# The share of v in the routing logits: embeddings as stationary operand in four column tiles, keys moving, then transposed back

## The chip, the core and the metric

The kernel runs on one core of a Trainium2 chip. A core has TensorE (PE, matrix products; its weight loads are listed as PEld), VectorE (DVE), ScalarE (ACT), GpSimd (POOL) and SyncE (SP, which here issues most DMA transfers). The metric is the device time of one execution in microseconds; less is better.

## What is computed

Windowed causal attention, then two mixture-of-experts layers in a row, each of which sends a token to its best expert.

```python
scores = np.where(mask, scale * q @ k.T + bias, -1e9)   # 4 batches, 8 heads, 576 tokens, head size 64
attn   = softmax(scores)                                # window of 128
x      = (attn @ v), heads side by side                 # 2304 tokens x 512
# layer 1, 8 experts of 512 x 1024 x 512
logits = normalised(x) @ normalised(expert_emb).T / tau
out[t] = gate[t] * (relu(x[t] @ w1[e]) @ w2[e]),  e = argmax(logits[t])
# layer 2: the same with logits = x @ w_gate
```

The logits of layer 1 are linear in the attention output before its normalisation. So the kernel doesn't compute them from x: it multiplies v by the embeddings first, one product for each head, and lets the attention weights sum these 8 numbers (E = 8) per token and head together with v.

## The kernel before

Attention goes through 80 units: 4 batches, each in two halves of 4 heads; in a half 5 blocks of queries (four of 128, one of 64) times 2 pairs of heads. Loop step s starts unit s and carries earlier units on: `scores` of unit s (q times k, tile `ps_s`, L604), exponentials of unit s-1 on ScalarE (tile `e`, L631), transposes of unit s-2 on PE (`ps_t`, L638), their copy to SBUF by ScalarE for unit s-3 (`et`, L644), split into two halves of the window by GpSimd (L656, L658), product with v of unit s-5 (`pv`, `ps_o`, L677 for the first block, L679 and L680 for the others), normalisation of unit s-6 on VectorE. A matrix product in fp32 is two records in the trace, each with its weight load; a transpose is one.

The schedule is manual: on each engine, and in each DMA queue, instructions stand in the order in which the code issues them. Semaphores order the engines among themselves. A transfer also waits for an earlier one: there are eight completion semaphores for the transfers (`DMAHW0` to `DMAHW7`), taken in turn over both queues, and a transfer waits for the one that used its semaphore before it.

`vts` holds, for two batches, v by tokens: for each of five blocks and 8 heads 64 values, a one, and 8 places for the product of v and the embeddings. A transfer (`load_v`, L486) fills v and the ones. `v_logits` fills the 8 places: `load_vT` (L490) brings a block of v transposed (4 groups of two heads, 128 partitions, 128 tokens); for each group one product with the block as stationary operand and the embeddings `enT` as moving operand (L523, tile `ps_v`, 128 tokens by 128 columns of which 16 are used); ScalarE's `put` (L509) moves the used ones to `vts`. `enT` has in each group the embeddings of the even head in the upper 64 rows, those of the odd head in the lower.

For the first batch `v_logits` is advanced by one `yield` in each step, after the exponentials and before the transposes; its first three vT blocks are loaded from SP's queue ahead of everything, the others by ScalarE's queue. For the later batches it is advanced at the end of each step, with some steps' pause between blocks. PSUM tiles of `ps_m` (two buffers, tag `misc`) are shared by `v_logits`, the gate and the transposes of the expert stage.

After attention the tokens are sent to a table by expert (L287), and the experts run, 16 of them in turn (L985 to L987 are their products).

Of the kernel before, what the change touches and what calls it, by code (L numbers as in the profile page):

```python
# [7 lines left out]
F32 = mybir.dt.float32  # L8
# [3 lines left out]
AF = mybir.ActivationFunctionType  # L12
# [6 lines left out]
B, H, S, D = 4, 8, 576, 64  # L19
T, DM, E, FF = B * S, H * D, 8, 1024  # L20
NB = 5
QB = [128, 128, 128, 128, 64]
# [3 lines left out]
KD, KF = DM // 128, FF // 128  # L26
# [11 lines left out]
NW = 4  # L38
JOIN = 224
NT = 5  # L40
NOV = 26

PAUSE = object()
# [41 lines left out]
class _Kernel:  # L85
# [16 lines left out]
    def consts(self):  # L102
# [18 lines left out]
        nc.gpsimd.iota(t("exbase", [128, E]), pattern=[[TP, E]], base=0, channel_multiplier=0, **it)  # L121
        nc.gpsimd.iota(t("ovt", [128, NOV]), pattern=[[1, NOV]], base=0, channel_multiplier=0, **it)
        nc.gpsimd.iota(t("ovs", [128, NOV]), pattern=[[128, NOV]], base=0, channel_multiplier=0, **it)
        yield
# [6 lines left out]
        for m in range(2):  # L131
# [18 lines left out]
            t(f"proc{m}", [128, E])  # L150
            t(f"oei{m}", [1, 2, NOV], I32)
            yield
# [7 lines left out]
    def gate_consts(self, rows, psum):  # L160

        nc, c, t = self.nc, self.c, self.const
        es = rows.tile([128, DM], F32, tag="row", name="es")[:E]
        en, e0 = t("en", [E, 1]), self.e0
        nc.scalar.activation(es, e0, AF.Square, accum_out=en)
        nc.gpsimd.tensor_tensor(en, en, c["half"][:E, :1], op=ALU.pow)
        yield
        nc.vector.tensor_scalar(en, en, 1e-6, None, ALU.add)
        nc.vector.tensor_tensor(en, en, c["taub"], op=ALU.mult)
        nc.vector.reciprocal(en, en)  # L170
        nc.vector.tensor_scalar(es, e0, en, None, ALU.mult)
        yield
        ep = psum.tile([128, 512], F32, tag="misc", name="ep")
        for kk in range(KD):
            nc.tensor.transpose(ep[:, kk * E : kk * E + E], es[:, kk * 128 : kk * 128 + 128], c["ident"][:E, :E])
        yield
        enT = t("enT", [128, KD * 2 * E + 128 - 2 * E])
        nc.vector.memset(enT, 0.0)
        for z in range(2):
            nc.vector.tensor_copy(enT[64 * z : 64 * z + 64, : KD * 2 * E].rearrange("p (k e) -> p k e", k=KD)[:, :, E * z : E * z + E],  # L180
                                  ep[64 * z : 64 * z + 64, : KD * E].rearrange("p (k e) -> p k e", k=KD))

    def bias(self, pool):
# [26 lines left out]
    def gate(self, m, l, nt, meta, slots, fix=None, valid=None, skip=None, lag=None, norm=None):  # L210
# [6 lines left out]
        def s3(name, dt=F32):  # L217
            return pool.tile([128, NT, E], dt, tag=f"g_{name}", name=f"g_{name}")[:, :nt]

        def s2(name, dt=F32):  # L220
            return pool.tile([128, NT], dt, tag=f"g_{name}", name=f"g_{name}")[:, :nt]

# [3 lines left out]
        def be(a):  # L226
            return a.unsqueeze(1).to_broadcast([128, nt, E])
# [31 lines left out]
        nc.tensor.matmul(pos, lhsT=c["ones"], rhs=be(acc), start=False, stop=True)  # L259
        cnt = pp[:, NT * E : NT * E + E]  # L260
        nc.tensor.matmul(cnt, lhsT=c["ones"], rhs=new, start=True, stop=True)
# [131 lines left out]
    def beyond(self, m, cnt):  # L393
# [4 lines left out]
        def t(name, shape, dt=F32):  # L398
            return gp.tile(shape, dt, tag=f"ov_{name}", name=f"ov_{name}")

        def by_e(x):
            return x.unsqueeze(2).to_broadcast([128, E, NOV])

        def by_t(x):
            return x.unsqueeze(1).to_broadcast([128, E, NOV])

        ov, nov = t("ov", [128, E]), t("nov", [128, E])
        og, o2 = t("og", [128, E, NOV]), t("o2", [128, E, NOV])
        nc.vector.tensor_tensor(ov, cnt, proc, op=ALU.subtract)
# [40 lines left out]
    def attention(self):  # L450
        nc, c = self.nc, self.c
        fifo, par = self.fifo, self.par
        W = D + 1 + E
        with ExitStack() as st:
            def P(name, bufs, **kw):
                return self.pool(st, name, bufs, **kw)

            kp = P("at_k", 1)
            wk, wk3, wk4 = P("at_w", 2), P("at_w3", 3), P("at_w4", 4)
            ps_s, ps_t, ps_o = P("ps_s", 2, space=PSUM), P("ps_t", 2, space=PSUM), P("ps_o", 2, space=PSUM)  # L460
            ps_m, rows = self.ps_m, self.rows
# [5 lines left out]
            vts = [kp.tile([128, NB * H * W + 128 - W], F32, name=f"vt{i}") for i in range(2)]  # L467

            vTs = {}

            def load_qk(i, y):

                b, f = halves[i]
                for a in range(2):
                    nc.sync.dma_start(qz[i % 2][y][64 * a : 64 * a + 64, a, :S], self.q[b, 2 * f + y, 64 * a : 64 * a + 64])
                nc.sync.dma_start(kz[i % 2][y], self.k[b, 2 * f + y])
# [7 lines left out]
            def load_v(b, x):  # L484
                n = QB[x]
                nc.sync.dma_start(vts[b % 2][:n, x * H * W : (x + 1) * H * W], self.v[b, x * 128 : x * 128 + n])  # L486

            def load_vT(b, x, eng=nc.scalar):
                vTs[b, x] = vT = wk3.tile([128, KD, 128], F32, tag="vT", name="vT")
                eng.dma_start(vT[:, :, : QB[x]], self.vT[b, :, :, x * 128 : x * 128 + QB[x]])  # L490

            def load(i):
                for y in range(2):
# [7 lines left out]

            def v_logits(b):

                for x in range(3):
                    if (b, x) not in vTs:
                        load_vT(b, x)
                def put(x, ps):
                    to = vts[b % 2][: QB[x], x * H * W : (x + 1) * H * W].rearrange("p (h w) -> p h w", h=H)
                    nc.scalar.activation(to[:, :, D + 1 :].rearrange("p (g z) e -> p g z e", z=2),  # L509
                                         ps[: QB[x]].rearrange("p (g f) -> p g f", g=KD)[:, :, : 2 * E].rearrange("p g (z e) -> p g z e", z=2), AF.Copy)  # L510

                for x, n in enumerate(QB):
                    for _ in range(4 if b and x % 2 == 0 else 0):
                        yield
                    if x:
                        put(x - 1, ps)
                        if x + 2 < NB:
                            load_vT(b, x + 2)
                    vT = vTs.pop((b, x))
                    ps = ps_m.tile([128, 512], F32, tag="misc", name="ps_v")  # L520
                    for g in range(KD):

                        nc.tensor.matmul(ps[:n, g * 128 : g * 128 + n], lhsT=vT[:, g, :n],  # L523
                                         rhs=c["enT"][:, g * 2 * E : g * 2 * E + n], start=True, stop=True)
                    yield
                put(NB - 1, ps)
                yield

            nc.vector.memset(self.const("half", [128, NB]), 0.5)
            ssqs = [self.const(f"ssq{i}", [128, NB]) for i in range(2)]  # L530
# [1 line left out]
            nc.scalar.activation(ssqs[0], ssqs[0], AF.Exp)  # L532
            load_qk(0, 0)
            self.gate_loads(rows)
            for x in range(2):
                load_v(0, x)
                load_vT(0, x, nc.sync)
            load_qk(0, 1)
            for x in range(2, 4):
                load_v(0, x)  # L540
                if x == 2:
                    load_vT(0, 2, nc.sync)
            load_v(0, 4)
            clear_q(0, 0, nc.vector)
            ident = self.const("ident", [128, 128])
# [35 lines left out]
            def gate_start():  # L581

                yield from gate
                yield
                yield from v_logits(0)

            vl = gate_start()
# [155 lines left out]
            for s in range(N + 7):  # L743
# [3 lines left out]
                if s < N:  # L747
                    i, j, p = units[s]
                    if (j, p) == (0, 1) and i and i + 1 < 2 * B:
                        par.add(load(i + 1))  # L750
                    if (j, p) == (3, 1) and halves[i] in [(b, 0) for b in range(B - 1)]:
                        par.add(load_vs(halves[i][0] + 1))
                    if (j, p) == (0, 0) and halves[i][1] == 1 and i + 1 < 2 * B:
                        par.add(v_logits(halves[i][0] + 1))
# [59 lines left out]
    def load_x(self, m, C, tab, key, src):  # L814
# [3 lines left out]
        nf, w = divmod(C, 128)  # L818
        meta = self.mp.tile([128, NT, 2], I32, tag="meta", name="meta")[:, :nt]
        if w:  # L820
# [6 lines left out]
        if m == 0:  # L827
            valid = self.mp.tile([128, NT], F32, tag="valid", name="valid")[:, :nt]
            skip = self.mp.tile([128, NT], F32, tag="skip", name="skip")[:, :nt]
        xj = None  # L830
# [439 lines left out]
```

## Time and profile before

| | |
|---|---|
| time, median of 3 runs | 723.21 us (722.36 to 723.77) |
| the profiled execution | 724.26 us, span 722.5 us |
| PE busy | 694.9 us, 96% of the span |
| DVE, ACT, POOL busy | 64%, 47%, 31% |
| granted clock of PE, mean | 0.986 |
| attention | about the first 185 us |

The time of an execution lies a little above its span, which goes from the first to the last instruction. Busy shares are means over stages of different kind, so they only say where to look.

### The profile page before, as it was taken

What the parts mean: (1) busy time and instruction counts of PE and PEld (TensorE: products, weight loads), DVE (VectorE), ACT (ScalarE), POOL (GpSimd) and SP (SyncE); (2) the same over time, 40 slices, a digit from 0 to 9 for tenths busy, and PEclk for the clock granted to TensorE, in tenths of its full rate; (3) what the DMA queues carried; (4) which work ended last, traced back from release to release, by engine and by line L of the source; (5) the groups of instructions that cost most, each with busy time, mean ns of one, the idle gap of its engine ahead of it and who ended that gap; (6) DMA issues with size and microseconds to landing.
All of it is one profiled execution on the core that took longest, in us unless ns stands there. A gap on an engine that the chain in (4) does not pass through costs nothing.

```text
span 722.5 us, 15371 instructions
## 1 busy us (share of the span) xinstructions
PE 694.9 (96%) x5215; PEld 673.5 (93%) x5215; DVE 462.7 (64%) x1611; ACT 339.2 (47%) x841; POOL 222.7 (31%) x372
## 2 busy tenths in 40 slices
PE   6799999998999999999999998999999999999996
PEld 5799999997989899999999998999999999999996
DVE  7366667587686756675767776763655555666671
ACT  3355455566425343544455453522544444455551
POOL 5233443545335222223233124133212212211311
PEclk9999999999998999999999999999999999999999
DMA  8725646431418545356545475016544444554700
GB/s 230 197 84 180 139 134 192 121 151 51 163 28 285 176 142 211 105 216 161 202 157 148 161 194 217 23 31 239 223 152 171 161 173 141 217 209 147 257 21 14
DMA packets 45135, 112.41 MB, mean 156 GB/s; under 512 B 15000, under 2 KB 23448, under 8 KB 36820
## 3 DMA queue, kind: packets, MB, share of 16 engines
q1 hardware_dynamic: 27588, 87.83, 35.8%
q0 software_dynamic: 8448, 18.93, 9.0%
q10 hardware_dynamic: 8976, 3.93, 2.4%
q8 instruction: 87, 1.43, 0.8%
q14 instruction: 36, 0.29, 0.2%
HBM read 97.58 MB, written 15.93 MB: 157 GB/s over the span
## 4 chain that ended last, share of the span: by engine, by line
PE 77%; DMA 11%; DVE 4%; issue 4%; POOL 2%; SPq 1%; ACT 0%; POOLq 0%; ACTq 0%; DVEq 0%
PE ps L985 17%; PE ps L986 16%; PE ps L987 16%; PE ps_s L604 8%; DMA xr<-xs,meta 7%; PE ps_o L679 4%; PE ps_o L680 4%; PE tpx L858 2%; PE ps_t L638 2%; PE ps_v L523 2%; PE tpy L931 2%; DVE wlo L805 2%; PE ps L982 1%; PE tpy L943 1%; DMA vt<-in_v 1%
## 5 line engine op out<-in xcount | busy, mean ns | idle before, releaser
L805 DVE TENSOR_TENSOR wlo<-raw,whi 128x512 fp32r<-128x512 f32 x256 | 169.5, 687 | 72.6 <-ACT whi L802 62.7
L985 PE MATMUL ps<-xh,whi 128*128 128x240 f32 (+12 forms) x544 | 165.7, 305 | 1.6 <-DVE tot L1050 0.9
L985 PE MATMUL ps<-hh,whi 128*128 128x240 f32 (+11 forms) x544 | 165.7, 305 | 0.0
L986 PE MATMUL ps<-hl,whi 128*128 128x240 f32 (+10 forms) x544 | 161.4, 297 | 0.9 <-DVE hl L1084 0.9
L986 PE MATMUL ps<-xl,whi 128*128 128x240 f32 (+10 forms) x544 | 161.1, 296 | 0.9 <-DVE xl L862 0.5
L987 PE MATMUL ps<-hh,wlo 128*128 128x240 f32 (+10 forms) x544 | 161.3, 297 | 0.0
L987 PE MATMUL ps<-xh,wlo 128*128 128x240 f32 (+10 forms) x544 | 160.7, 295 | 0.5 <-issue 0.5
L802 ACT ACTIVATE whi<-raw 128x512 fp32r<-128x512 f32 x256 | 151.5, 623 | 3.0 <-DMA raw<-in_moe_w 3.0
L1079 ACT ACTIVATE hh<-ps 128x256 fp32r<-128x256 f32 (+10 forms) x136 | 57.2, 421 | 114.3 <-PE ps L987 107.4
L985 PEld LDWEIGHTS ps<-xh,whi 128*128 128x128 f32 x544 | 102.7, 189 | 2.2 <-ACT yT L1116 1.1
L986 PEld LDWEIGHTS ps<-hl,whi 128*128 128x128 f32 x544 | 103.5, 190 | 1.3 <-DVE hl L1084 1.3
L986 PEld LDWEIGHTS ps<-xl,whi 128*128 128x128 f32 x544 | 102.7, 189 | 1.8 <-DVE xl L862 1.0
L985 PEld LDWEIGHTS ps<-hh,whi 128*128 128x128 f32 x544 | 103.4, 190 | 0.5 <-ACT hh L1079 0.2
L987 PEld LDWEIGHTS ps<-xh,wlo 128*128 128x128 f32 x544 | 102.6, 189 | 1.0 <-issue 0.9
L987 PEld LDWEIGHTS ps<-hh,wlo 128*128 128x128 f32 x544 | 103.3, 190 | 0.1
L844 POOL DMA_INDIRECT xr<-xs,meta x50 | 53.8, 1076 | 157.7 <-DMA meta<-tab 106.1
L1084 DVE SCALAR_TENSOR_TENSOR hl<-ps,hh 128x256 fp32r<-128x256 f32 (+10 forms) x136 | 63.3, 467 | 60.2 <-ACT hh L1079 53.5
L1116 ACT ACTIVATE yT<-ps 128x256 f32<-128x256 f32 (+10 forms) x68 | 28.8, 423 | 126.0 <-PE ps L987 106.0
L604 PE MATMUL ps_s<-kz,qz 128*128 128x256 f32 (+1 forms) x320 | 81.5, 379 | 5.4 <-DMA kz<-in_k 5.4
L604 PEld LDWEIGHTS ps_s<-kz,qz 128*128 128x128 f32 x320 | 55.0, 195 | 9.5 <-DVE vt L551 5.4
L287 POOL DMA_INDIRECT out<-y,meta x26 | 31.6, 1215 | 93.0 <-DVE y L944 88.2
L631 ACT ACTIVATE e<-z,mn 128x128 f32<-128x128 f32 x160 | 54.6, 391 | 5.5 <-DVE mn L622 5.3
(205 smaller groups left out, 1034.0 us busy)
## 6 DMA issues: line engine op xcount, KB each, us to landing
raw<-in_moe_w SPq DMA_DIRECT2D x64, 1024.0 KB
vt<-in_v SPq DMA_DIRECT2D x16, 292.0 KB
qz<-in_q SPq DMA_DIRECT2D x32, 144.0 KB
kz<-in_k SPq DMA_DIRECT2D x16, 288.0 KB
xs<-xt SPq DMA_DIRECT2D x16, 256.0 KB
vT<-in_vT ACTq DMA_DIRECT2D x13, 256.0 KB
xr<-xs,meta POOLq DMA_INDIRECT x50
vT<-in_vT SPq DMA_DIRECT2D x3, 256.0 KB
```

The source lines that it names most:

```text
L287: k = self.nc.gpsimd.indirect_dma_start(dst, bass.IndirectOffsetOnAxis(ap=idx, axis=0), src, None, bounds_check=last, oob_is_err=False)
L604: nc.tensor.matmul(ps[:, a, k1:], lhsT=qz[i % 2][p][:, a, j * 128 : j * 128 + 128], rhs=kz[i % 2][p][:, m0 + k1 : m0 + 256], start=True, s ...
L631: nc.scalar.activation(e[:, a], z[:, a], AF.Exp, bias=mn[:, a : a + 1], scale=-1.0)
L679: nc.tensor.matmul(o, lhsT=e0[:, a], rhs=cols(j - 1), start=True, stop=False)
L802: nc.scalar.activation(hi[:, sl], rw[:, sl], AF.Copy)
L805: (eng or eng2).tensor_tensor(lo[:, sl], rw[:, sl], hi[:, sl].bitcast(F32), op=ALU.subtract)
L844: k = nc.gpsimd.indirect_dma_start(x[:n], None, src, bass.IndirectOffsetOnAxis(ap=meta[:n, i, 0:1], axis=0), bounds_check=src.shape[0] - 1 ...
L985: nc.tensor.matmul(ps[:, :v], lhsT=ah, rhs=Bh[:, kk, :v], start=kk == 0, stop=False)
L986: nc.tensor.matmul(ps[:, :w], lhsT=ah, rhs=Bl[:, kk, :w], start=False, stop=False)
L987: nc.tensor.matmul(ps[:, :w], lhsT=al, rhs=Bh[:, kk, :w], start=False, stop=kk == kn - 1)
L1079: nc.scalar.activation(hh[:, mm], ps, AF.Relu)
L1084: nc.vector.scalar_tensor_tensor(hl[:, mm], ps, 0.0, hh[:, mm].bitcast(F32), op0=ALU.max, op1=ALU.subtract)
```

## The change

The two operands of the v products change places. `enT` becomes 4 groups of 32 columns (16 of them used) and is the stationary operand; the block of v transposed moves. Group g writes PSUM partitions 32g to 32g+31, so that four products fill the 128 partitions of one tile, each in its own tile of 32 columns of the array. The result then has tokens along the free dimension. So ScalarE copies it to SBUF (`vl`, L524), PE transposes it in pieces of 128 tokens (L528, tile `ps_vt`), and `put` (L536) moves the used parts to `vts` as before. Blocks are 256, 256 and 64 tokens wide; vT has two buffers in place of three. The pipeline in `v_logits` becomes one step longer: products, then copy and transposes, then `put`.

```diff
+PM = 512
...
-        enT = t("enT", [128, KD * 2 * E + 128 - 2 * E])
+        enT = t("enT", [128, KD, 32])
         nc.vector.memset(enT, 0.0)
...
+            VB = ((0, 256), (256, 256), (512, 64))
+
             def load_vT(b, x, eng=nc.scalar):
-                vTs[b, x] = vT = wk3.tile([128, KD, 128], F32, tag="vT", name="vT")
-                eng.dma_start(vT[:, :, : QB[x]], self.vT[b, :, :, x * 128 : x * 128 + QB[x]])
+                k0, n = VB[x]
+                vTs[b, x] = vT = wk.tile([128, KD, 256], F32, tag="vT", name="vT")
+                eng.dma_start(vT[:, :, :n], self.vT[b, :, :, k0 : k0 + n])
...
             def v_logits(b):
 
-                for x in range(3):
+                for x in range(2):
                     if (b, x) not in vTs:
                         load_vT(b, x)
...
-                for x, n in enumerate(QB):
-                    for _ in range(4 if b and x % 2 == 0 else 0):
+                pss = {}
+
+                def products(x):
+
+                    n = VB[x][1]
+                    vT = vTs.pop((b, x))
+                    pss[x] = ps = ps_m.tile([128, PM], F32, tag="misc", name="ps_v")
+                    for g in range(KD):
+                        nc.tensor.matmul(ps[32 * g : 32 * g + 32, :n], lhsT=c["enT"][:, g], rhs=vT[:, g, :n], start=True, stop=True)
+
+                def turned(x):
+                    n = VB[x][1]
+                    sb = wk.tile([128, 256], F32, tag="vl", name="vl")
+                    nc.scalar.activation(sb[:, :n], pss[x][:, :n], AF.Copy)
+                    pss[x] = ps = ps_m.tile([128, PM], F32, tag="misc", name="ps_vt")
+                    for y in range(0, n, 128):
+                        k = min(128, n - y)
+                        nc.tensor.transpose(ps[:k, y : y + 128], sb[:, y : y + k], c["ident"])
+
+                def put(x):
+                    k0, n = VB[x]
+                    ps = pss.pop(x)
+                    for y in range(0, n, 128):
...
+                for x in range(len(VB) + 2):
+                    for _ in range(3 if b and x < len(VB) else 0):
                         yield
-                    if x:
-                        put(x - 1, ps)
-                        if x + 2 < NB:
+                    if x >= 2:
+                        put(x - 2)
+                    if 0 < x <= len(VB):
+                        turned(x - 1)
+                    if x < len(VB):
+                        products(x)
+                        if x + 2 < len(VB):
                             load_vT(b, x + 2)
...
-            for x in range(2):
-                load_v(0, x)
-                load_vT(0, x, nc.sync)
+            load_v(0, 0)
+            load_vT(0, 0, nc.sync)
+            load_v(0, 1)
             load_qk(0, 1)
-            for x in range(2, 4):
-                load_v(0, x)
-                if x == 2:
-                    load_vT(0, 2, nc.sync)
+            load_v(0, 2)
+            load_vT(0, 1, nc.sync)
+            load_v(0, 3)
             load_v(0, 4)
```

On PE, steps 3 to 6 of the first batch, before (`ps_s` scores, `ps_t` transposes, `ps_v` products of v, `ps_o` product with v):

```order
L604 MATMUL ps_s<-kz_114,qz_110 128x256 x2
L523 MATMUL ps_v<-enT,vT 128x128 x4
L638 MATMUL ps_t<-ident,e 128x128 x2
L604 MATMUL ps_s<-kz_114,qz_110 128x192 x2
L523 MATMUL ps_v<-enT,vT 128x128 x4
L638 MATMUL ps_t<-ident,e 128x128 x2
L604 MATMUL ps_s<-kz_115,qz_111 128x256 x2
L523 MATMUL ps_v<-enT,vT 128x128 x4
L677 MATMUL ps_o<-vt_118,et 128x128 x2
```

The same place on PE in the changed program (its line numbers are 22 higher from the scores on):

```order
L626 MATMUL ps_s<-kz_114,qz_110 128x256 x2
L519 MATMUL ps_v<-vT,enT 32x256 x4
L660 MATMUL ps_t<-ident,e 128x128 x2
L626 MATMUL ps_s<-kz_114,qz_110 128x192 x2
L528 MATMUL ps_vt<-ident,vl 128x128 x2
L519 MATMUL ps_v<-vT,enT 32x256 x4
L660 MATMUL ps_t<-ident,e 128x128 x2
L626 MATMUL ps_s<-kz_115,qz_111 128x256 x2
L528 MATMUL ps_vt<-ident,vl 128x128 x2
L519 MATMUL ps_v<-vT,enT 32x64 x4
L699 MATMUL ps_o<-vt_118,et 128x128 x2
```

The last products of the batch have moved one step ahead, and transposes of ScalarE's copy now stand between scores and products.

On ScalarE at that place, before, from the exponentials of step 3 on (the brackets name the semaphores that an instruction waits for; DMAHW7 was last used by the load of the last block of v):

```order
L631 ACTIVATE e<-z,mn 128x128 [waits DVE_49] x2
L644 ACTIVATE et<-ps_t 128x256 [waits PE_49]
L631 ACTIVATE e<-z,mn 128x128 [waits DVE_49] x2
L509 ACTIVATE vt_118<-ps_v 128x8x8 [waits DMAHW5_49]
L490 DMA vT<-in_vT 128x4x128 [waits DMAHW7_49,DMAHW6_49]
L644 ACTIVATE et<-ps_t 128x256 [waits PE_49]
```

And in the changed program (DMAHW3 was last used by the load of v's third block):

```order
L653 ACTIVATE e<-z,mn 128x128 [waits DVE_49] x2
L494 DMA vT<-in_vT 128x4x64 [waits DMAHW6_49,DMAHW3_49,PE_49]
L666 ACTIVATE et<-ps_t 128x256 [waits PE_49]
L653 ACTIVATE e<-z,mn 128x128 [waits DVE_49] x2
L524 ACTIVATE vl<-ps_v 128x256
L666 ACTIVATE et<-ps_t 128x256 [waits PE_49]
L653 ACTIVATE e<-z,mn 128x128 [waits DVE_49] x2
L536 ACTIVATE vt_118<-ps_vt 128x8x8 [waits DMAHW5_49]
L536 ACTIVATE vt_118<-ps_vt 128x8x8 [waits DMAHW7_49]
L524 ACTIVATE vl<-ps_v 128x256
```

The only load of vT that ScalarE still issues in the first batch has moved ahead by one copy and one pair of exponentials, waits for PE's first products instead of the last block of v, and is followed by copies of the products.

On SP's queue, loads for the first batch, before:

```order
L486 DMA vt_118<-in_v 128x584
L490 DMA vT<-in_vT 128x4x128
L486 DMA vt_118<-in_v 128x584
L490 DMA vT<-in_vT 128x4x128
L475 DMA qz_111<-in_q 64x576 x2
L476 DMA kz_115<-in_k 128x576
L486 DMA vt_118<-in_v 128x584
L490 DMA vT<-in_vT 128x4x128
L486 DMA vt_118<-in_v 128x584
L486 DMA vt_118<-in_v 64x584
```

After:

```order
L487 DMA vt_118<-in_v 128x584
L494 DMA vT<-in_vT 128x4x256
L487 DMA vt_118<-in_v 128x584
L476 DMA qz_111<-in_q 64x576 x2
L477 DMA kz_115<-in_k 128x576
L487 DMA vt_118<-in_v 128x584
L494 DMA vT<-in_vT 128x4x256
L487 DMA vt_118<-in_v 128x584
L487 DMA vt_118<-in_v 64x584
```

Three blocks of vT have become two of double width, so that 512 of 576 tokens are loaded from here in place of 384; up to the second pair of heads' k the bytes are the same.

## Rows read from the trace of the kernel before

**Rows 1.** The page: busy time, and the chain's shares by engine.

```profile
PE 694.9 (96%) x5215; PEld 673.5 (93%) x5215; DVE 462.7 (64%) x1611; ACT 339.2 (47%) x841; POOL 222.7 (31%) x372
...
PE 77%; DMA 11%; DVE 4%; issue 4%; POOL 2%; SPq 1%; ACT 0%; POOLq 0%; ACTq 0%; DVEq 0%
```

**Rows 2.** Windows of attention: length, busy time by engine, clock, DMA share, GB/s.

```profile
30.00:60.00 30.00, 30.00 (x224) 28.79 (x224) 17.89 (x124) 16.20 (x54) 10.66 (x61) 1.00 0.39 117
...
100.00:155.00 55.00, 55.00 (x412) 52.25 (x411) 37.56 (x223) 30.70 (x103) 23.33 (x49) 1.00 0.57 176
```

**Rows 3.** Timeline of PE around a 64-wide tile: start, length, what.

```profile
65.68 0.38 PE L638 MATMUL ps_t<-ident,e 128*128 128x128 f32 x2
65.90 1.03 PE L604 MATMUL ps_s<-kz,qz 128*128 128x256 f32 x4
66.76 0.61 PE L677 MATMUL ps_o<-vt,et 128*128 128x128 f32 x4
67.21 0.38 PE L638 MATMUL ps_t<-ident,e 128*128 128x128 f32 x2
67.52 0.68 PE L523 MATMUL ps_v<-enT,vT 128*64 128x64 f32 x8
...
69.09 0.39 PE L679 MATMUL ps_o<-vt,e 128*128 128x128 f32 x2
```

**Rows 4.** Timeline of PE around a 128-wide tile.

```profile
96.20 1.06 PE L523 MATMUL ps_v<-enT,vT 128*128 128x128 f32 x8
...
97.10 1.03 PE L604 MATMUL ps_s<-kz,qz 128*128 128x256 f32 x4
```

**Rows 5.** Groups of ScalarE, 30 to 155 us: busy, mean ns, idle before.

```profile
L644 ACT ACTIVATE et<-ps_t 128x256 f32<-128x256 f32 x60 | 22.7, 378 | 32.6 <-PE ps_t L638 30.6 <-DMA qz<-in_q 1.2 <-POOL wid L141 0.4
...
L509 ACT ACTIVATE vt<-ps_v 128x64 f32<-128x64 f32 x12 | 2.6, 214 | 0.0
```

**Rows 6.** Timeline of PE, first 30 us.

```profile
12.03 1.16 PE L523 MATMUL ps_v<-enT,vT 128*128 128x128 f32 x8 [0.23 <-DVE enT L180]
...
13.24 0.88 PE L604 MATMUL ps_s<-kz,qz 128*128 128x192 f32 x4
...
17.48 1.03 PE L604 MATMUL ps_s<-kz,qz 128*128 128x256 f32 x4
22.69 1.67 PE L523 MATMUL ps_v<-enT,vT 128*128 128x128 f32 x8 [4.18 <-DMA vT<-in_vT]
...
26.28 1.15 PE L604 MATMUL ps_s<-kz,qz 128*128 128x256 f32 x4
...
29.18 1.03 PE L604 MATMUL ps_s<-kz,qz 128*128 128x256 f32 x4
```

**Rows 7.** The chain that ended last, first 34 us: start, length, what.

```profile
9.46 6.69 DMA vt<-in_v
16.23 6.32 DMA vT<-in_vT
...
25.21 0.43 PE ps_o L679 x2
...
28.68 0.22 PE ps_o L679 x2
```

**Rows 8.** Timeline of ScalarE, 12 to 17 us.

```profile
12.90 0.69 ACT L631 ACTIVATE e<-z,mn 128x128 f32<-128x128 f32 x2 [1.54 <-DVE mn L622]
...
14.56 0.69 ACT L631 ACTIVATE e<-z,mn 128x128 f32<-128x128 f32 x2 [0.70 <-DVE mn L622]
...
16.23 0.64 ACTq L490 DMA_DIRECT2D vT<-in_vT  x1
```

**Rows 9.** The window behind that wait, columns as in rows 2.

```profile
22.60:26.00 3.40, 3.31 (x17) 3.35 (x18) 0.00 (x0) 0.00 (x0) 0.00 (x0) 0.57 1.08 291
```

**Rows 10.** The chain behind attention's full stretch.

```profile
167.91 5.66 DMA tab<-meta,sl
...
189.83 5.28 DMA raw<-in_moe_w
```

More of the change, by code (lines that the diff above doesn't have):

```diff
@@ L176, in gate_consts @@
         yield
-        enT = t("enT", [128, KD * 2 * E + 128 - 2 * E])
+        enT = t("enT", [128, KD, 32])
         nc.vector.memset(enT, 0.0)
         for z in range(2):
-            nc.vector.tensor_copy(enT[64 * z : 64 * z + 64, : KD * 2 * E].rearrange("p (k e) -> p k e", k=KD)[:, :, E * z : E * z + E],
+            nc.vector.tensor_copy(enT[64 * z : 64 * z + 64, :, E * z : E * z + E],
                                   ep[64 * z : 64 * z + 64, : KD * E].rearrange("p (k e) -> p k e", k=KD))
@@ L502, in v_logits @@
             def v_logits(b):
-                for x in range(3):
+                for x in range(2):
                     if (b, x) not in vTs:
                         load_vT(b, x)
[L507 to L510, printed above, removed]
@@ L512, in v_logits @@
-                for x, n in enumerate(QB):
-                    for _ in range(4 if b and x % 2 == 0 else 0):
-                        yield
-                    if x:
-                        put(x - 1, ps)
-                        if x + 2 < NB:
-                            load_vT(b, x + 2)
[L519 to L524, printed above, removed]
+                pss = {}
@@ new lines, in put @@
+                def put(x):
+                    k0, n = VB[x]
+                    ps = pss.pop(x)
+                    for y in range(0, n, 128):
+                        k, xx = min(128, n - y), (k0 + y) // 128
+                        to = vts[b % 2][:k, xx * H * W : (xx + 1) * H * W].rearrange("p (h w) -> p h w", h=H)
+                        nc.scalar.activation(to[:, :, D + 1 :].rearrange("p (g z) e -> p g z e", z=2),
+                                             ps[:k, y : y + 128].rearrange("p (g f) -> p g f", g=KD)[:, :, : 2 * E].rearrange("p g (z e) -> p g z e", z=2), AF.Copy)
@@ L525, in v_logits @@
+                for x in range(len(VB) + 2):
+                    for _ in range(3 if b and x < len(VB) else 0):
+                        yield
+                    if x >= 2:
[5 more added lines that the diff above has]
+                        if x + 2 < len(VB):
+                            load_vT(b, x + 2)
                     yield
-                put(NB - 1, ps)
@@ L527, in v_logits @@
-                yield
             nc.vector.memset(self.const("half", [128, NB]), 0.5)
```

## The prediction

> **What bounds the kernel now.** I read the page's busy table and chain first. TensorE (PE) is busy for 96% of the span and holds 77% of the chain that ended last; DMA holds 11% [rows 1]. The change touches attention only, so I asked for the windows of that stage: from 30 to 155 us PE is busy without a gap at full clock, while VectorE and ScalarE have room [rows 2]. There every microsecond of PE work is a microsecond of time. The exception is the first 30 us. PE's timeline shows the embedding products of v's fourth tile (the fourth call of L523) starting only at 22.69, after 4.18 us of idle, released by a transfer of vT [rows 6]. The chain says why: the last tile of v lands 6.69 us after 9.46; only then (16.23) is the load of vT's fourth tile issued from ScalarE's queue, and it takes 6.32 us [rows 7]. [...] So two places matter: what the v products cost PE in the full stretch, and what happens in the first 30 us.
>
> **What the products cost, before.** An fp32 matmul shows as two records. A 128-wide tile (8 records) takes from 96.20 to 97.10, 0.90 us, or 0.112 a record [rows 4]. The 64-wide tile is dear: from the transposes ahead of it (67.21) to the first work behind the scores (69.09) is 1.88 us; without it transposes and scores take 0.22 + 0.86 = 1.08 (65.68, 65.90, 66.76) [rows 3]. So it costs 0.80. Eight records of half width should take 8 x 0.056 = 0.45; the other 0.35 is the price of going to a 64-column stationary operand and back. A batch costs 4 x 0.90 + 0.80 = 4.40 us.
>
> **And after.** A batch has two 256-wide groups and one 64-wide group of four products, each into its own 32 columns, then four full transposes and one of 64 tokens.
> - Each 256-wide record streams twice as long as a 128-wide one: 0.216 (scores: four such records in 0.86 [rows 3]). Eight in a row would be 1.73.
> - No row shows products in different column tiles, so overlap is bounded: none (1.73) from the row above, and full, 2 x 0.216 = 0.43 for the two records of one product. I choose between them. The two records of one product use the same columns and cannot overlap; in every row records start in program order. So record 2 of one product can overlap record 1 of the next, and no more: five streams in place of eight, 5 x 0.216 = 1.08. For the 64-wide group: 0.45, 0.28 or 0.11.
> - Going into 32-column tiles and back: 0.35 for each group, by the 64-wide row, the nearest [rows 3]. The lone 64-token transpose also has a 64-column stationary operand: another 0.35. Zero is the lower bound.
> - Transposes are one record: 0.11 each, five per batch, 0.55 [rows 3].
> A batch after: 2 x (1.08 + 0.35) + 0.28 + 0.35 + 0.55 + 0.35 = 4.39 us. That is no change. With full overlap 2.92 (-1.48), with none 5.86 (+1.46). If changing tiles cost nothing, a batch would be 1.40 cheaper (four times 0.35) in the chosen case.
>
> [...]
>
> **Other engines in batches 1 to 3.** ScalarE gains a copy of the products (128x256: 378 ns by the copies of L644) and keeps the puts at 214 ns each [rows 5]; it drops two of five load issues of about 0.6 us. The new wait is PE's transposes on ScalarE's copy. There the generator is advanced at the end of a step, so the copy needs products some four steps old (one step old for the last group) and has the step's scores and P.V ahead of it on PE, 1.75 us, while ScalarE has about 0.35 + 0.68 + 0.43 + 0.35 = 1.8 us to do, from the previous step's transposes on. I price this at nothing; if that cover fails it is some 0.3 us a group, 2.7 us in nine. The third vT load now waits on ScalarE's queue for the products (two buffers), but the next item of that queue waits for later PE work anyway.
>
> **The first 30 us, step by step.** The embeddings still arrive at 12.03 [rows 6]. Here the generator is advanced mid-step, so PE meets the new copy early.
> - Products 0: 12.03 + 1.43 = 13.46. Transposes, then scores of step 4: 14.35. ScalarE meanwhile: exponentials to 13.6, issue of the last vT load (0.64), copy, exponentials (ready at 14.56 before [rows 8], now to about 15.3), product copy, about 15.65. PE waits 1.3 us.
> - Two transposes, products 1, transposes, scores of step 5: 15.65 + 0.22 + 1.43 + 0.22 + 0.86 = 18.4. ScalarE starts only when the step's transposes are done (17.5): copy, exponentials, two puts, product copy, 19.4. PE waits 1.0.
> - Products 2 need the last vT load. It is issued at about 13.7, no longer behind the last tile of v, and lands by the row's 6.32 us at about 20.0. Then 0.63 for the group, 0.66 for P.V and transposes, 0.86 for scores: 22.2. ScalarE's round: 23.0. Lone transpose 0.46, P.V 0.89, transposes 0.22, scores 0.86, P.V and transposes 1.11: scores of step 8 start at 26.5.
> Before they start at 29.18 [rows 6]. So the start gains **2.7 us**: one idle time of 4.18 and the slow stretch (3.4 us at 0.57 lose 1.5 [rows 9]) go, waits of 1.3, 1.0, 0.7 and 0.8 come, and the later products move forward into them. With no overlap between tiles it gains about 2.2, with full overlap 2.9, since ScalarE and the load set most of it.
>
> **Does it reach the end?** From 161 the chain leaves PE for table writes and loads (5.66 us for the last write, 5.28 for weights) [rows 10]. These follow attention's own instructions, so I let the gain pass whole; stretches at the lower clock may fall elsewhere, some 1.5 us each by the row above.
>
> **Sum.** The profiled execution took 724.26 us, 1.05 above the median of 723.21; its span is 722.5. -2.7 at the start, 3 x 0.0 later: 721.5 beside 724.26, **720.5** beside the median.
>
> **Rivals.**
> - **Full overlap.** Should all four tiles stream at once, both records, 3 x -1.48 and -2.9: -7.3, 715.9. [...]
> - **No overlap (slower).** If each product waits for the one before it, 3 x 1.46 - 2.2 = +2.2: 725.4. Its place is the nine groups of batches 1 to 3. It decides from some 6.8 streams of 8 left in a row: each stream beyond five costs about 0.49 us a batch, 1.5 in three, against 2.7. That the records are in program order speaks for it; that the tiles share no columns, against.
> - **The clock falls again.** The new waits at the start are shorter than 4.18 but close together; a fall like that of [rows 9] gives back 1.5: 722.0, no change that can be told.
> - **The start does not gain.** If the last load lands as late as before (22.7) despite its earlier issue, or the 512 KB loads push back v's own tiles, the 2.7 goes: 723.2.
>
> **Chances.** The forecast 0.36 (own range 718.8 to 721.7), full overlap 0.20, no overlap 0.20, clock 0.14, no gain at the start 0.10. A measurement of this kernel can tell about 0.2%, 1.4 us, from no change: below 721.8 is faster, above 724.6 slower. Faster: the forecast, full overlap and a little of the clock case, 0.58. Slower: most of the no-overlap case and little else, 0.17. The rest, 0.25, is no change. The range goes from full overlap to no overlap, with little beyond: 715.5 to 725.5.
>
> **What would show it.** On PE, from the first product of a 256-wide group to the scores behind it: 1.4 us if right, near 0.8 with full overlap, above 2 with none. Around a lone 64-token transpose, 0.35 beyond its 0.11. At the start no idle time near 4 us on vT, two or three near 1 us on ScalarE's copy, scores of step 8 at 26.5, and full clock from 22 to 27. From 30 to 155, PE without gaps. The forecast is wrong if tiles overlap otherwise than in pairs, if the last load lands later than 20, or if PE waits for ScalarE's copies in batches 1 to 3.

## The result, and the profile after

The changed kernel took 713.93 us (median of 4 runs, 710.88 to 718.84), the kernel before beside it 723.49 (4 runs, 722.36 to 726.54): ratio 0.9856, 95% interval 0.9821 to 0.989. That is 9.6 us faster, below the range of the prediction and 2 us below its rival of full overlap (715.9; the interval reaches up to 715.5). The profiled execution is the slowest of the four: 718.84 us, span 717.1.

From the page: busy time, and the chain's shares by engine.

```profile
PE 686.6 (96%) x5171; PEld 660.0 (92%) x5171; DVE 463.4 (65%) x1611; ACT 343.0 (48%) x853; POOL 225.5 (31%) x372
...
PE 76%; DMA 11%; DVE 6%; issue 4%; POOL 1%; ACT 1%; POOLq 0%; DVEq 0%; ACTq 0%
```

PE is busy 8.3 us less than before and still for 96% of a shorter span [rows 1]. Windows of attention, columns as in [rows 2]:

```profile
30.00:60.00 30.00, 30.00 (x227) 27.30 (x226) 18.52 (x126) 17.82 (x61) 9.60 (x56) 1.00 0.44 139
...
100.00:150.00 50.00, 49.63 (x379) 45.93 (x378) 37.15 (x222) 29.98 (x100) 23.27 (x50) 1.00 0.57 168
```

So attention is still bounded by PE at full clock: what its instructions save there is time. PE's timeline around a 256-wide group, a 64-wide group, the lone 64-token transpose behind it, and 192-wide scores with no group ahead of them:

```profile
44.32 0.38 PE L528 MATMUL ps_vt<-ident,vl 128*128 128x128 f32 x2
44.63 0.64 PE L519 MATMUL ps_v<-vT,enT 128*32 128x256 f32 x8
45.20 0.92 PE L626 MATMUL ps_s<-kz,qz 128*128 128x192 f32 x4
45.95 0.38 PE L701 MATMUL ps_o<-vt,e 128*128 128x128 f32 x2
...
52.77 0.38 PE L528 MATMUL ps_vt<-ident,vl 128*128 128x128 f32 x2
53.09 0.32 PE L519 MATMUL ps_v<-vT,enT 128*32 128x64 f32 x8
53.34 1.13 PE L626 MATMUL ps_s<-kz,qz 128*128 128x256 f32 x4
54.30 0.38 PE L701 MATMUL ps_o<-vt,e 128*128 128x128 f32 x2
...
55.41 0.27 PE L528 MATMUL ps_vt<-ident,vl 128*64 128x128 f32 x1
55.52 1.03 PE L626 MATMUL ps_s<-kz,qz 128*128 128x256 f32 x4
56.39 0.38 PE L701 MATMUL ps_o<-vt,e 128*128 128x128 f32 x2
...
144.18 0.82 PE L626 MATMUL ps_s<-kz,qz 128*128 128x192 f32 x4
144.83 0.38 PE L701 MATMUL ps_o<-vt,e 128*128 128x128 f32 x2
```

Starts are to be read here, since the lengths of neighbours overlap. From the products' start (44.63) to the scores behind them (45.20) is 0.57 us; the forecast would have shown 1.4, full overlap 0.8, none over 2. From the transposes ahead to the first work behind the scores is 1.63 (44.32 to 45.95). Two transposes are 0.22 of that, four 192-wide score records 0.65 (144.18 to 144.83): the group costs **0.76**, which is 0.43 for two 256-wide streams and 0.33 for going into 32-column tiles and back. The 64-wide group: 1.53 - 0.22 - 0.86 = **0.45**, 0.11 and 0.34. The lone transpose has a 64-column stationary operand and takes 0.11 with no gap on either side.

The trace's single records of the group at 44.63 say how (start in us of each of the eight):

```
44.630  44.636  44.643  44.650     44.870  44.876  44.883  44.890
```

Four start 7 ns apart, and 0.24 us after the first, when one 256-wide stream (0.216, [rows 3]) has run, the other four. The records don't say which tile they belong to; that these are the first records of all four products and then the second ones is the reading that fits two streams in 0.43. It takes for granted that two records in the same columns don't run side by side, as in the rows: the four 256-wide score records from 65.90 on [rows 3] start 0.216 to 0.218 apart.

The start: PE's timeline, then ScalarE's, then the chain.

```profile
11.39 0.64 PE L519 MATMUL ps_v<-vT,enT 128*32 128x256 f32 x8
...
14.94 0.44 PE L528 MATMUL ps_vt<-ident,vl 128*128 128x128 f32 x2 [1.46 <-ACT vl L524]
...
16.69 1.91 PE L626 MATMUL ps_s<-kz,qz 128*128 128x256 f32 x4
18.45 0.63 PE L528 MATMUL ps_vt<-ident,vl 128*128 128x128 f32 x2
19.54 0.32 PE L519 MATMUL ps_v<-vT,enT 128*32 128x64 f32 x8 [0.46 <-DMA vT<-in_vT]
...
22.11 0.30 PE L528 MATMUL ps_vt<-ident,vl 128*64 128x128 f32 x1 [0.53 <-ACT vl L524]
...
25.34 1.03 PE L626 MATMUL ps_s<-kz,qz 128*128 128x256 f32 x4
```

```profile
12.57 0.64 ACTq L494 DMA_DIRECT2D vT<-in_vT  x1
...
14.53 0.36 ACT L524 ACTIVATE vl<-ps_v 128x256 f32<-128x256 f32 x1
```

```profile
12.57 6.83 DMA vT<-in_vT
19.54 0.32 PE ps_v L519 x8
```

The wait of 4.18 [rows 6] is gone; waits of 1.46, 0.46 and 0.53 stand in its place. The last load of vT is issued at 12.57 in place of 16.23 [rows 7] and takes 6.83. Scores of step 8 start at 25.34, before at 29.18: -3.84. The clock still falls, earlier, with the scores of step 5 inside. The window, columns as in [rows 2]:

```profile
15.50:18.90 3.40, 3.40 (x16) 1.78 (x8) 0.16 (x1) 1.46 (x6) 0.86 (x5) 0.50 1.14 238
```

What PE waited for up to 165 us (total, times, longest):

```profile
PE ps_s L626 <- DVE vt L573: 5.2, 1, 5.2
PE ps_vt L528 <- ACT vl L524: 2.0, 2, 1.5
PE ps_v L519 <- DMA vT<-in_vT: 0.7, 2, 0.5
PE ps_s L626 <- DVE mn L644: 0.2, 1, 0.2
```

The 5.2 lies ahead of the kernel's first scores. Both waits for ScalarE's copy are those of the start: in batches 1 to 3 there is none.

**The balance.** Read from the starts of scores on PE's timeline (before, after): step 8 at 29.18 and 25.34; step 75 at 166.93 and 158.23; the first product of the expert layers at 187.34 and 177.04. So 3.8 at the start, 4.9 in steps 8 to 75, 1.6 at the end of attention (a wait of 0.88 for ScalarE's exponentials at 170.81 in the trace of before is not there after; in set 3 below this stretch takes 18.6 before and 19.1 after, so no such gain): 10.3. From 724.26 that gives 714.0, the median. The profiled execution lost some 4.9 of it again behind attention, above all where the second expert layer gathers its rows. The stretch with 200 of its products takes 36.2 us (from 407) in place of 31.3 (from 416), at a granted clock of 0.93 in place of 0.98. PE's longest wait there, after and then before:

```profile
PE tpx L880 <- DMA xr<-xs,meta: 5.5, 1, 5.5
```

```profile
PE tpx L858 <- DMA xr<-xs,meta: 2.6, 1, 2.6
```

The three other runs (710.88 to 714.07) lie at that 714.0 or below it.

### The profile page after: what moved, and what is told of

It reads as the page before. It is cut to its first block, busy times and chain, and to the rows that moved or that the text cites. A ratio compares the mean times of both kernels' runs of the same rounds, so it can differ in the third digit from the quotient of the medians.

```text
span 717.1 us, 15267 instructions
## 1 busy us (share of the span) xinstructions
PE 686.6 (96%) x5171; PEld 660.0 (92%) x5171; DVE 463.4 (65%) x1611; ACT 343.0 (48%) x853; POOL 225.5 (31%) x372
## 4 chain that ended last, share of the span: by engine, by line
PE 76%; DMA 11%; DVE 6%; issue 4%; POOL 1%; ACT 1%; POOLq 0%; DVEq 0%; ACTq 0%
PE ps L1007 17%; PE ps L1008 16%; PE ps L1009 16%; PE ps_s L626 8%; DMA xr<-xs,meta 8%; PE ps_o L701 3%; PE ps_o L702 3%; PE tpx L880 3%; PE ps_t L660 2%; DMA vT<-in_vT 2%; PE tpy L953 2%; DVE wlo L827 1%; PE tpy L965 1%; PE ps_o L699 1%; PE ps L1004 1%
## 5 line engine op out<-in xcount | busy, mean ns | idle before, releaser
L866 POOL DMA_INDIRECT xr<-xs,meta x50 | 55.7, 1114 | 156.9 <-DMA meta<-tab 82.4
L626 PEld LDWEIGHTS ps_s<-kz,qz 128*128 128x128 f32 x320 | 55.3, 196 | 12.4 <-DVE vt L573 5.2
```

Of the source, the lines that this page charges most:

```text
L626: nc.tensor.matmul(ps[:, a, k1:], lhsT=qz[i % 2][p][:, a, j * 128 : j * 128 + 128], rhs=kz[i % 2][p][:, m0 + k1 : m0 + 256], start=True, s ...
L866: k = nc.gpsimd.indirect_dma_start(x[:n], None, src, bass.IndirectOffsetOnAxis(ap=meta[:n, i, 0:1], axis=0), bounds_check=src.shape[0] - 1 ...
```

## The experiments

Each set ran on one chip with runs of the kernel before among them; ratios are to those. The marks are of each profiled execution: start of step 8's scores, and the time from step 15's to step 75's (the first of the nine groups of batches 1 to 3 lies ahead of step 15). In the first profiles they were 29.18 and 123.7 before, 25.34 and 118.9 after. The times in the expectations of set 1 are those of the first chip, where the kernel before took 723.5; in set 1 it took 726.6, so differences from it compare, and not the times.

| kernel | us, median (runs) | ratio, 95% interval | step 8 at | steps 15 to 75 |
|---|---|---|---|---|
| **set 1** before | 726.61 (30) | | | |
| changed, again | 720.47 (9) | 0.9907 (0.9877 to 0.9938) | 27.53 | 118.7 |
| no column tiles | 727.84 (12) | 1.0028 (0.9994 to 1.0061) | 31.13 | 125.0 |
| old products, early loads | 722.05 (12) | 0.9927 (0.9902 to 0.9953) | 22.71 | 124.2 |
| halves by group | 719.41 (10) | 0.9911 (0.9883 to 0.9939) | 27.94 | 118.9 |
| **set 2** before | 728.88 (9) | | | |
| early third load | 715.48 (5) | 0.9805 (0.9765 to 0.9845) | 25.67 | 118.8 |
| two blocks | 713.72 (5) | 0.9795 (0.9761 to 0.9828) | 23.45 | 117.7 |
| first batch old | 715.69 (5) | 0.9812 (0.9763 to 0.9861) | 23.48 | 119.0 |
| both | 715.11 (5) | 0.9801 (0.9753 to 0.9848) | 23.22 | 118.0 |
| **set 3** before | 728.84 (17) | | | |
| before, profiled | 729.71 (12) | 1.002 (0.9987 to 1.0053) | 30.48 | 123.7 |
| changed, third time | 720.54 (6) | 0.9896 (0.9851 to 0.9942) | 26.74 | 118.7 |
| two blocks again | 712.67 (6) | 0.9792 (0.9755 to 0.983) | 23.51 | 117.7 |
| two blocks, late turn | 711.56 (6) | 0.978 (0.9738 to 0.9823) | 22.25 | 117.7 |

**Is it the overlap of the tiles?** Unaltered, the changed kernel was expected to do this:

> The changed kernel unaltered, for a profile and times beside the experiments: 714 us, 711 to 717; the executions differ by where the clock falls and by the gathers between the two layers.

It took 720.47, above the 711 to 717 expected, and 6.1 less than the kernel before (4.5 to 8.9). The 60 steps are those of the first profile; step 8 is 2.2 later, with a wait of 2.1 for the load of vT where the first profile has 0.46.

The same form without column tiles: 128 columns of stationary operand, zero but for the group's own, four products added up in PSUM.

```diff
-        enT = t("enT", [128, KD, 32])
+        enT = t("enT", [128, KD, 128])
...
-                        nc.tensor.matmul(ps[32 * g : 32 * g + 32, :n], lhsT=c["enT"][:, g], rhs=vT[:, g, :n], start=True, stop=True)
+                        nc.tensor.matmul(ps[:, :n], lhsT=c["enT"][:, g], rhs=vT[:, g, :n], start=g == 0, stop=g == KD - 1)
```

> The changed kernel with each group of embeddings in a 128-column stationary operand, zero but for its own 16 columns, and the four products summed in PSUM: the same work after it, but no column tiles, so nothing can overlap. If the gain is the overlap: a 256-wide group takes 1.73 us in place of 0.57, a batch 2.4 us more, some 8.5 us in four: 722.5 us. If the gain comes from the loads at the start and from fewer issues, not from PE: 714 to 716.

PE's timeline of it:

```profile
51.08 0.38 PE L529 MATMUL ps_vt<-ident,vl 128*128 128x128 f32 x2
51.29 1.89 PE L520 MATMUL ps_v<-vT,enT 128*128 128x256 f32 x8
53.02 0.81 PE L627 MATMUL ps_s<-kz,qz 128*128 128x192 f32 x4
53.67 0.38 PE L702 MATMUL ps_o<-vt,e 128*128 128x128 f32 x2
```

A group now takes 1.73 (51.29 to 53.02): eight streams of 0.216 in a row, with no gap ahead of it (51.08 + 0.22) and none in the scores (0.65). A 64-wide group takes 0.84 from its start to the scores, where with tiles it takes 0.25. Steps 15 to 75 take 6.3 us more than with tiles and 1.3 more than before: in the batches the whole saving is the overlap. In all this form takes 7.4 more than the changed kernel (8.5 was expected). The start is lost as well. ScalarE's timeline and PE's waits:

```profile
17.16 0.64 ACTq L495 DMA_DIRECT2D vT<-in_vT  x1
17.85 0.38 ACT L667 ACTIVATE et<-ps_t 128x256 f32<-128x256 f32 x1 [3.61 <-issue]
```

```profile
PE ps_vt L529 <- ACT vl L525: 4.8, 3, 3.8
```

The load on ScalarE's queue is issued at 17.16 here, where the changed kernel had it at 12.57; the copy behind it is 4.2 late (18.71 for 14.53), and PE waits 3.8 for it. By the trace's semaphore events it is issued here when the fourth block of v has landed (17.09), in the changed kernel when the third has (12.47), whose completion semaphore it takes there; in the trace of before it is issued at 16.23, when the last block, ahead of it on its semaphore, has landed (16.15). That it takes another semaphore here is the author's reading of these times. So this wait is the load's and not the tiles'; the clean comparison is that of the batches.

Does the overlap hang on the order in which products are written? Each product in two halves, all of one tile's records ahead of the next tile's:

```diff
-                        nc.tensor.matmul(ps[32 * g : 32 * g + 32, :n], lhsT=c["enT"][:, g], rhs=vT[:, g, :n], start=True, stop=True)
+                        for y in range(0, n, n // 2):
+                            nc.tensor.matmul(ps[32 * g : 32 * g + 32, y : y + n // 2], lhsT=c["enT"][:, g], rhs=vT[:, g, y : y + n // 2], start=True, stop=True)
```

> The changed kernel with each product in two halves of the width, issued group by group (both halves of group 0, then of group 1, and so on). If each column tile takes its records as soon as it is free, whatever stands between them in the program: the group keeps its 0.57 us, 714 us. If records start strictly in program order and only the two records of one product are spread: a group takes about 1.5 us, some 1 us more in eight wide groups, 721 to 722.

```profile
47.26 0.67 PE L520 MATMUL ps_v<-vT,enT 128*32 128x128 f32 x16
47.85 0.92 PE L627 MATMUL ps_s<-kz,qz 128*128 128x192 f32 x4
```

0.59 a group in place of 0.57, and the same time: no. (Step 8 is 0.4 later; PE waits 3.3 for a copy behind the load's issue at 15.53, which follows the landing of the third block of v at 15.46.) The sixteen records start in four rounds (47.256, .389, .498, .608), in each round four of them 13 ns apart. If only neighbours in the program could overlap, 13 of the 16 streams of 0.108 would stand in a row, 1.4 us. The step within a round, 13 ns in place of 7, fits as well: the first records of neighbouring tiles are four records apart in the program, in place of two. So by this reading each column tile works through its own records while the others do theirs.

**What is the start worth by itself?** The products of before, with all five loads of the first batch issued from SP's queue early, and the later batches' five loads at once:

```diff
...
-                for x in range(3):
+                for x in range(NB):
...
-                        if x + 2 < NB:
-                            load_vT(b, x + 2)
...
-                if x == 2:
-                    load_vT(0, 2, nc.sync)
+                load_vT(0, x, nc.sync)
...
+            load_vT(0, 4, nc.sync)
```

> The kernel before with all five loads of vT for the first batch issued from SP at the start, and for the later batches at once. If the gain has two halves: the start alone is mended, 3.5 to 5 us, 718.5 to 720. If the loads are all of it: 714.

Step 8 starts at 22.71, 6.5 us before that of the kernel before in its first profile, with the clock full from 10 to 30 us (four 256-wide score records take 0.86, 17.06 to 17.92), and steps 15 to 75 take the 124 us of before. But the five issues of the next batch hold ScalarE's queue. ScalarE's timeline, and PE's waits:

```profile
27.33 5.07 ACTq L490 DMA_DIRECT2D vT<-in_vT  x5
32.51 0.38 ACT L642 ACTIVATE et<-ps_t 128x256 f32<-128x256 f32 x1 [4.82 <-DMA vT<-in_vT]
```

```profile
PE ps_t L636 <- ACT e L629: 1.3, 1, 1.3
```

That gives back 1.7 by step 15 (38.53, before 43.26: -4.7). 4.6 us faster in all (3.4 to 7.1), about the start's 4.7: a gain at the start alone reaches the end, without one in the batches.

**What is left of the waits at the start?** The 64-wide block in a buffer of its own, loaded from SP at the start:

```diff
-                vTs[b, x] = vT = wk.tile([128, KD, 256], F32, tag="vT", name="vT")
+                vTs[b, x] = vT = (wk, wk, kp)[x].tile([128, KD, (256, 256, 64)[x]], F32, tag=f"vT{x // 2}", name="vT")
...
+            load_vT(0, 2, nc.sync)
```

> The changed kernel with the 64-wide block of vT in a buffer of its own, loaded from SP's queue at the start, so that ScalarE's queue issues no load in the first batch and waits for none. If that issue holds ScalarE's copies up at the start: scores of step 8 at 25 to 25.5 us, no wait of PE for vT, 1.5 to 2 us less than the changed kernel. If the waits come from the copies alone: no change against it.

The third group no longer waits for its load, but step 8 starts at 25.67, no earlier than the 25.34 of the first profile and 1.1 to 1.9 before those of the two others: the load was only one of the things late there. PE still waits 1.5 and 0.5 for ScalarE's copy, and the clock still falls (0.71 from 18 to 22 us). Fewer, larger blocks:

```diff
-            VB = ((0, 256), (256, 256), (512, 64))
+            VB = ((0, 256), (256, 320))
...
```

> The changed kernel with blocks of 256 and 320 tokens in place of 256, 256 and 64: the start as in the run before, and one group of products less per batch. If entering the column tiles costs as in the trace of the changed kernel (a 64-wide group some 0.45 us, of which 0.1 streams): 0.3 us a batch less on top, 2.5 to 3 us less than the changed kernel in all. If PE then waits for ScalarE's longer copy: the same as the run before.

```profile
42.74 0.75 PE L519 MATMUL ps_v<-vT,enT 128*32 128x320 f32 x8
43.42 0.92 PE L626 MATMUL ps_s<-kz,qz 128*128 128x192 f32 x4
```

A 320-wide group takes 0.68, 0.11 more than a 256-wide one; the third group, with its two changes of tiles (0.34) and its load, is gone. Steps 15 to 75 take 1.0 to 1.2 less than the changed kernel's, step 8 starts at 23.45 (the granted clock is 1.00 from 10 to 30 us in two blocks again, whose step 8 is at 23.51). In the first batch the old products, the keys as stationary operand, and their puts, all blocks loaded from SP:

```diff
+            def v_first():
...
+                for x, n in enumerate(QB):
...
+                    for g in range(KD):
+                        nc.tensor.matmul(ps[:n, g * 128 : g * 128 + n], lhsT=vT[:, g, o : o + n],
+                                         rhs=c["enW"][:, g * 2 * E : g * 2 * E + n], start=True, stop=True)
+                    yield
...
-                yield from v_logits(0)
+                yield from v_first()
```

> The first batch with the keys stationary as before the change, all loads of vT at the start from SP; the other batches as changed. If the start and the later batches are independent: scores of step 8 at 22.7 us as in the old products with early loads, steps 15 to 75 in 119 us as in the changed kernel, 10 to 11 us less than the kernel before. If column tiles were the better choice in the first batch too: not better than the run before the last.

> Both: first batch with the keys stationary, two blocks of 256 and 320. 11 to 12 us less than the kernel before if the parts add up.

PE doesn't wait for vT or ScalarE's copy at all, and step 8 starts at 23.48 and 23.22 (22.7 was expected), as with two blocks: at the start the new form takes no longer than the old one once its loads come in time. Two blocks and the old first batch together gain 13.8 (11 to 12 was expected), no more than two blocks alone (15.2).

**One chip, one set.** The kernel before, the changed one and two blocks again, and two blocks with the first batch's copy, transposes and next products issued at the end of their step:

```diff
+                    if b == 0:
+                        yield
...
-                yield from gate
+                for _ in gate:
+                    yield
+                    yield
+                yield
...
+                next(vl, None)
```

> The kernel before, unaltered, profiled on the chip of the three runs below. Scores of step 8 near 29.2 us, 60 steps from step 15 to 75 in 123.7 us, the time of before within 0.2%. If the chip and not the kernel made the differences between the profiles compared so far, these marks would move here.

> The changed kernel unaltered on the same chip. Full overlap of the four column tiles: steps 15 to 75 in 118.9 us, 4.7 to 4.8 us below before, and scores of step 8 between 25.3 and 27.5 us by how late the 64-wide block's load lands; 6 to 10 us below before in all. Rival, that the gain of attention is lost again where the gather of the second layer waits: below 4 us.

> Blocks of 256 and 64 keys. One group, one turn of modes and one load less in each batch: steps 15 to 75 in 117.7 us, scores of step 8 at 23.5 us; 3 to 5 us below after_same_chip. Rival, that the start alone gains and the rest is hidden: 2 us below it.

> two_blocks with the copy, the transposes and the next products of the first batch issued at the end of their step, behind work that TensorE can do meanwhile. If the waits for ScalarE's copy (1.16 and 0.74 us) are on the path: no wait of TensorE for vl before step 8, scores of step 8 at 22 to 22.5 us, 1 to 1.5 us below two_blocks_again. Rival, that TensorE then waits for the next thing as long (the last block's products or their copy come later): same time as two_blocks_again within 0.4 us.

The kernel before shows the same 123.7 for its 60 steps, but step 8 at 30.48 where 29.2 was expected: that mark moves by 1.3 us between two profiles of one kernel on two chips, so a difference of that size between sets says little. Two blocks again has blocks of 256 and 320 tokens, as in its diff above, and not the 256 and 64 of its expectation.

PE's wait for the copy in the first batch, two blocks and then late turn:

```profile
PE ps_vt L528 <- ACT vl L524: 2.2, 2, 1.5
```

```profile
PE ps_vt L528 <- ACT vl L524: 0.9, 1, 0.9
```

Step 8 moves by 1.26 (the two profiles of two blocks have 23.45 and 23.51), as expected, though one wait of 0.9 stays; the medians differ by 1.1, less than their intervals. The changed kernel came out 8.3 us below before (4.2 to 10.9), two blocks 16.2 (12.4 to 17.9). Of the 7.9 between them the first expert product shows 3.3 (178.45 and 175.13); the rest lies behind attention: from that product to the end the two profiled executions take 542.8 and 534.1 us. There PE's waits move from execution to execution of one kernel too (the same stretch of the kernel before: 535.2 in its first profile, 541.1 in set 3), so this part is not explained.

## Why the prediction was wrong

**The step that failed** is the choice for the 256-wide groups: "record 2 of one product can overlap record 1 of the next, and no more: five streams in place of eight, 5 x 0.216 = 1.08". It was 0.43. That records start in program order was read from rows in which all products use the same columns; it was taken over to products in different tiles, where the records of the trace start four at a time. The other half of the choice, that records in the same columns don't overlap, held in what was measured (eight of them take 1.73 without column tiles, 8 x 0.216). The rival of full overlap held: four products of two records each take two streams, with starts 7 ns apart. The prediction gave this 0.20.

**Term by term, for a batch.** Two 256-wide groups: 2 x (1.08 + 0.35) = 2.86 forecast, 1.52 measured. 64-wide group: 0.28 + 0.35, measured 0.45. Transposes: 0.55, as forecast. The lone transpose: 0.35 forecast, 0 measured. Sum 4.39 forecast, 2.52 measured; against 4.40 before that saves 1.88, or 5.6 in three batches. Of the 1.87 between the sums, 1.47 is the overlap, 0.35 the lone transpose, 0.05 the change of tiles. Steps 8 to 75 show 4.9; 0.23 of the rest is a wait for vT at 116.27, and 0.37 is lost at 146 us in the step that holds the routing's small matmuls.

**The price of changing tiles** was right where it applies: 0.33 and 0.34 for 32-column groups, the 0.35 of the 64-wide tile [rows 3]. It is not paid by the lone transpose, whose stationary operand has 64 columns too (0.11 us, with no gap on either side); why not, no run shows.

**The start**: -3.84 where -2.7 was forecast, -3.74 in set 3. Of the 1.1 more, 0.6 is there from the first products on, at 11.39 in place of 12.03. Right was the kind of the waits: 1.3, 1.0, 0.7 for the load and 0.8 were forecast, 1.46, none, 0.46 and 0.53 came. Wrong was the clock: it was to stay full from 22 to 27 and did (1.00), but it falls from 15.5 to 18.9 (0.50). It cost little there, because the load that PE meets at 19.54 was on its way meanwhile (12.57 + 6.83 = 19.40).

**Does it reach the end?** Yes: 10.3 us at the first expert product and 9.6 in the medians. In set 1 it was 6.1 (4.5 to 8.9), in set 3 8.3, with 8.4 at the first expert product of set 3's profiles. The first profile's 10.3 is also more than the 7.3 of the rival of full overlap: 0.4 in the batches, 0.9 at the start, and 1.6 at the end of attention that no term held and set 3 doesn't repeat. The 1.6 is luck.

**ScalarE in batches 1 to 3**, priced at nothing: no wait, as forecast. Nine waits of 0.3 would have cost 2.7.

## What to carry to other kernels

Here four products with few output columns, each in a column tile of its own, cost one product's streams (0.43, where without column tiles a row of them takes 1.73), plus about 0.33 for each group that goes into the tiles and back; so make few, wide groups (320 and 256 in place of 256, 256 and 64 gained another 1.0 to 1.2 us in steps 15 to 75). What must be turned back costs a copy on another engine: issue the work that needs it later, where TensorE has other work (in the first batch its waits for the copy went from 2.2 to 0.9 us). And before an order read from rows is taken over to a new form, ask whether the rows have that form in them: no row of before had products in different tiles.

## What the runs showed of the hardware

Four fp32 products in four 32-column tiles take two streams (0.43 us for 256 columns), and as the trace is read above, the records of one tile run in a row and those of different tiles side by side, even where the program has all of one tile's products ahead of the next tile's (0.59 us a group in place of 0.57). A lone transpose with 64 columns costs nothing beyond its 0.11 us that the trace shows, while a group in 32-column tiles costs 0.33 beyond its streams. A load whose issue waits on ScalarE's queue holds that engine's copies with it (4.8 us of idle time for five issues), and the same load was issued at 12.57 and at 17.16 us in two kernels, 0.10 and 0.07 after the landing of another block of v (12.47 and 17.09). And the stretch behind attention takes 534 to 543 us in these profiles, 535.2 and 541.1 in two of the kernel before, which is a spread as large as what this change is worth.
